# Query pairs one loop step later, and the feed of the bursts with more room at both ends of sweep two

## The chip, the cores and the metric

One core of a Trainium2 chip. The time is the device time of one launch in microseconds (us); the runs shown are medians over several executions. The engines are TensorE (PE; its weight loads are listed apart as PEld), VectorE (DVE), ScalarE (ACT), GpSimd (POOL) and SyncE (SP), which here only issues DMAs.

## The reference

x is 2048 rows of 512 values, all float32.

```python
qkv = x @ wqkv                                   # 32 heads of 16
pq, pk = q @ w_phi, k @ w_phi                    # per head 16 x 16
phi_q = concat(softmax(pq), softmax(-pq))        # 32 features
phi_k = concat(softmax(pk), softmax(-pk))
kv, z = phi_k^T v, sum over rows of phi_k        # over all 2048 rows
a = ((phi_q kv) / (phi_q z + 1e-6)) @ wo
h = relu(x @ w1 + b1); h = h * h                 # 1792 hidden columns
b = h @ w2 + b2
g = sigmoid(sum(x * gate_w))
out = g * a + (1 - g) * b
```

kv and z need all rows before the first query can be used; this divides the kernel into two sweeps over the rows.

## The kernel before, in words

A float32 product is made of three fp32r matmuls (mm3): each operand is split into a high part, which ACT rounds (`xh`, `hh`, `oh`, ...), and a low part, which DVE subtracts (`xl`, `hl`, `ol`, ...).

The rows are taken in 4 blocks of 512, the hidden columns in 14 chunks of 128. Each sweep passes over all blocks with 7 of the 14 chunks. So the main loop has 2 x 4 x 7 = 56 steps t. In each, PE does one `u` group of 12 matmuls (do_up, for the chunk that is needed two steps on, LAG = 2) and one `d` group of 12 (down, into four PSUM accumulators); ACT and DVE make the squared relu between them (hidden). At the end of a block the accumulators are added into rows (L597), the evictions below: in sweep one these go out as `part`, in sweep two they are added to what sweep one left, and either finish or meet the attention part.

All other work hangs in between at half steps: at(s, f, ...) puts f into half step s, where 2t comes ahead of the `u` group of step t and 2t + 1 between `u` and `d`. A framework then orders each engine's queue by these program positions and its own estimate of when operands and buffers are free, with some pieces (exps, the splits of `oh` and `ol`, the evictions) given a higher priority.

Sweep one (half steps 0 to 55) carries, beside the FFN, for each 128 rows the products `k` and `v`, the exponentials of `k`, and phi_k^T v (`kvps`, which holds one PSUM bank, so that one bank is left for all else). Near its end the weights for the queries are made: do_fold("q", k) at half steps 49 to 52, each a small product in that one bank (`foldq`) and a split (`wqh`, `wql`). Also near its end the next block's x rows, the first of sweep two, are split (x_ready, `xh` and `xl`, two 128-row pieces in a half step), from buffers that x_fetch has loaded; do_w loads and splits `wo` (`woh`, `wol`).

Sweep two (56 to 111) carries the queries. A pair p of row chunks goes through

- do_q, twice, two half steps apart: the product `q`, exponentials on DVE and ACT, the denominator (POOL makes `ez`, DVE `dz`, `den`), the scaled features, and transposed: DVE transposes 32 x 32 blocks into `tb`, and 16 copies bring these to their place in `phiT`, 4 by ACT and 12 by DMAs that SP issues (L303). `phiT` has one buffer, so the copies of a pair wait for the burst of the pair before.
- do_n, ten half steps after the first do_q: the burst `num`, 32 small matmuls on `phiT` into two PSUM banks, and the split of the result (`oh`, `ol`). The first two matmuls of the burst run ahead of the other 30.
- finish, twice, from twelve half steps after the first do_q: the product `att` with `wo`, and its addition to the row (L490).

`q`, `num` and `att` share two PSUM banks in turn. do_x(b) loads and splits the x rows of the later blocks at half steps 63, 72 and 82. A block of sweep two ends at 69, 83, 97 and 111.

```python
for p in range(NB * NC // 2):
    n, s = 2 * p, 54 + 6 * p
    q, late = divmod(n, NC)[0], p == NB * NC // 2 - 1
```

Of the kernel before, what the change touches and what calls it, by code (L numbers as in the profile page):

```python
# [20 lines left out]
NB = S // SB  # L21
NC = SB // P
# [10 lines left out]
def tile_gated_mix(ctx: ExitStack, tc: tile.TileContext, xT, xn, wqT, wkT, wphi, wv, wo, w1, b1, w2, b2, gw, out):  # L33
# [464 lines left out]
    SL = 2 * NFH  # L498
    steps = {}

    def at(slot, f, *a):
        steps.setdefault(int(slot), []).append(lambda: f(*a))
# [13 lines left out]
    for b in range(NB):  # L516
        for c in range(NC):
            s = b * SL + 3 * c - 3 if b else 3
            at(s, gate_load, b * NC + c)
            at(s + 3 if b else 8 + c, gate_chunk, b * NC + c)  # L520
        at(b * SL + 4, x_fetch, b + 1)
        for k in range(NK):
            at(b * SL + 7 + k // 2, x_ready, b + 1, k)
        for c in range(NC):
            n = b * NC + c
            s = 5 + 2.9 * n
            at(s, do_k, b, c)
            at(s + 2, do_v, b, n, c)
            if c % 2:
                at(s + 5, do_kv, n - 1)  # L530
# [9 lines left out]


    for p in range(NB * NC // 2):
        n, s = 2 * p, 54 + 6 * p
        q, late = divmod(n, NC)[0], p == NB * NC // 2 - 1
        at(s + 12 - 2 * late, finish, n, n % NC)
        at(s + 13 - 2 * late, finish, n + 1, n % NC + 1)
        at(s, do_q, NB + q, n, n % NC)
        at(s + 2, do_q, NB + q, n + 1, n % NC + 1)
        at(s + 10 - 2 * late, do_n, p)
    for b, slot in enumerate((7, 2, -2)):  # L550
        at((NB + b) * SL + slot, do_x, NB + b + 1)

# [12 lines left out]
    for t, (sw, b, i) in enumerate(work_list):  # L565
# [17 lines left out]
        for c in range(NC):  # L583
            n = b * NC + c
# [62 lines left out]
```

## Time and profile before

| | |
|---|---|
| median of 3 runs | 526.96 us (526.89 to 527.18) |
| the profiled execution | 527.2 us, of which the span from first to last instruction is 525.4 |
| busy, share of the span | PE 98%, PEld 79%, DVE 69%, ACT 45%, POOL 15% |
| granted TensorE clock | 0.999 of full speed |
| DMA queue of SP and ACT | 30328 packets, 44.20 MB, 26.7% of 16 engines' span |

Read it so: matmuls are pipelined and their ends are modelled, so one matmul row is shown with about 390 ns while the next one starts 227 ns later; PE's 98% says that it hardly ever lay idle. A row of the timeline is start, duration, engine, line, operation, output <- inputs, shapes, count, and in brackets the idle time of the engine before it with what ended it.

### The profile page before, as it was taken

What the parts mean: (1) busy time and instruction counts of PE and PEld (TensorE: products, weight loads), DVE (VectorE), ACT (ScalarE), POOL (GpSimd) and SP (SyncE); (2) the same over time, 40 slices, a digit from 0 to 9 for tenths busy, and PEclk for the clock granted to TensorE, in tenths of its full rate; (3) what the DMA queues carried; (4) which work ended last, traced back from release to release, by engine and by line L of the source; (5) the groups of instructions that cost most, each with busy time, mean ns of one, the idle gap of its engine ahead of it and who ended that gap; (6) DMA issues with size and microseconds to landing.
All of it is one profiled execution on the core that took longest, in us unless ns stands there. A gap on an engine that the chain in (4) does not pass through costs nothing.

```text
span 525.4 us, 8895 instructions
## 1 busy us (share of the span) xinstructions
PE 517.2 (98%) x3462; PEld 415.9 (79%) x3462; DVE 360.5 (69%) x606; ACT 236.5 (45%) x405; POOL 78.1 (15%) x60
## 2 busy tenths in 40 slices
PE   8999999999999999999999999999999999999997
PEld 3887888888888888888788878787878878787785
DVE  3569764463636646765879897997788887779323
ACT  5665534344334444354754473553434352535230
POOL 1001211111111111210103121112021111112000
PEclk9999999999999999999999999999999999999999
DMA  8844131120201031521255113234103311022102
GB/s 290 308 142 142 61 93 48 42 81 21 94 9 41 8 133 42 160 72 31 80 167 197 41 42 121 68 105 133 45 13 111 109 32 30 24 91 81 48 1 80
DMA packets 30834, 45.16 MB, mean 86 GB/s; under 512 B 5704, under 2 KB 12360, under 8 KB 30792
## 3 DMA queue, kind: packets, MB, share of 16 engines
q1 hardware_dynamic: 30328, 44.20, 26.7%
q8 instruction: 27, 0.44, 0.3%
q10 hardware_dynamic: 432, 0.39, 0.2%
q14 instruction: 15, 0.12, 0.1%
q0 software_dynamic: 32, 0.01, 0.0%
HBM read 29.89 MB, written 8.39 MB: 73 GB/s over the span
## 4 chain that ended last, share of the span: by engine, by line
PE 73%; DVE 12%; SPq 4%; issue 3%; ACT 2%; DMA 2%; POOL 2%; DVEq 0%; ACTq 0%; POOLq 0%
PE u L70 7%; PE u L72 7%; PE u L71 7%; PE d L71 7%; PE d L72 7%; PE d L70 7%; SPq L303 4%; PE v L70 3%; PE v L71 2%; PE v L72 2%; PE k L70 2%; PE k L72 2%; PE k L71 2%; PE att L70 2%; POOL ez L277 2%
## 5 line engine op out<-in xcount | busy, mean ns | idle before, releaser
L349 ACT ACTIVATE r<-u,b1c 128x512 f32<-128x512 f32 x56 | 38.5, 687 | 140.1 <-PE u L72 139.7
L70 PE MATMUL d<-w2h,hh 128*128 128x512 f32 x224 | 87.4, 390 | 0.0
L71 PE MATMUL d<-w2l,hh 128*128 128x512 f32 x224 | 87.4, 390 | 0.0
L72 PE MATMUL d<-w2h,hl 128*128 128x512 f32 x224 | 87.2, 389 | 0.0
L70 PE MATMUL u<-xh,w1h 128*128 128x512 f32 x220 | 86.9, 395 | 0.0
L72 PE MATMUL u<-xh,w1l 128*128 128x512 f32 x220 | 85.9, 390 | 0.0
L71 PE MATMUL u<-xl,w1h 128*128 128x512 f32 x220 | 85.7, 390 | 0.0
L65 DVE TENSOR_TENSOR hl<-r,hh 128x512 fp32r<-128x512 f32 x56 | 43.1, 769 | 53.4 <-ACT hh L62 53.2
L277 POOL TENSOR_TENSOR ez<-e,z 128x512 f32<-128x512 f32 x32 | 41.4, 1315 | 188.7 <-ACT e L249 164.5
L258 POOL TENSOR_TENSOR e<-e,r 128x1024 f32<-128x1024 f32 x16 | 34.5, 2158 | 206.6 <-DVE r L254 131.7
L252 DVE TENSOR_REDUCE sm<-e 128x64 f32<-128x1024 f32 x32 | 39.0, 1218 | 32.9 <-ACT e L249 32.9
L70 PEld LDWEIGHTS u<-xh,w1h 128*128 128x128 f32 x220 | 41.3, 188 | 12.1 <-ACT hh L62 1.6
L70 PEld LDWEIGHTS d<-w2h,hh 128*128 128x128 f32 x224 | 42.1, 188 | 8.7
L72 PEld LDWEIGHTS d<-w2h,hl 128*128 128x128 f32 x224 | 42.1, 188 | 8.7
L71 PEld LDWEIGHTS d<-w2l,hh 128*128 128x128 f32 x224 | 42.1, 188 | 8.6
L72 PEld LDWEIGHTS u<-xh,w1l 128*128 128x128 f32 x220 | 41.3, 188 | 9.3 <-DVE w1l L65 0.7
L71 PEld LDWEIGHTS u<-xl,w1h 128*128 128x128 f32 x220 | 41.3, 188 | 8.2
L249 ACT ACTIVATE e<-e 128x1024 f32<-128x1024 f32 x32 | 33.7, 1055 | 21.8 <-DVE e L247 17.3
L301 ACT ACTIVATE phiT<-tb 32x256 f32<-32x256 f32 x64 | 26.5, 414 | 34.5 <-DVE tb L295 33.8
L62 ACT ACTIVATE hh<-r 128x512 fp32r<-128x512 f32 x56 | 35.3, 630 | 1.5
L350 ACT ACTIVATE r<-r 128x512 f32<-128x512 f32 x56 | 35.2, 629 | 1.2
L597 DVE SCALAR_TENSOR_TENSOR row<-d,rest,row 128x512 f32<-128x512 f32 (+1 forms) x33 | 22.4, 732 | 6.2 <-PE d L72 6.1
(100 smaller groups left out, 872.3 us busy)
## 6 DMA issues: line engine op xcount, KB each, us to landing
in<-in_w SPq DMA_DIRECT2D x24, 256.0 KB, 2.7
phiT<-tb SPq DMA_DIRECT2D x192, 32.0 KB, 1.8
xin<-in_xT SPq DMA_DIRECT2D x20, 256.0 KB, 4.6
xn<-in_xn SPq DMA_DIRECT2D x16, 256.0 KB, 2.8
part<-row SPq DMA_DIRECT2D x16, 256.0 KB, 3.0
row<-part SPq DMA_DIRECT2D x16, 256.0 KB, 3.1
out<-row SPq DMA_DIRECT2D x15, 256.0 KB, 2.3
in<-in_xT SPq DMA_DIRECT2D x12, 256.0 KB, 4.3
```

Source lines behind the costliest of these rows:

```text
L62: i = nc.scalar.activation(hi, src, AF.Copy)
L65: st["low"] = elo.tensor_tensor(lo, src, hi.bitcast(F32), ALU.subtract)
L70: nc.tensor.matmul(o, ah[:, sa], bh[:, sb], start=first, stop=False)
L71: nc.tensor.matmul(o, ah[:, sa], bl[:, sb], start=False, stop=False)
L72: return nc.tensor.matmul(o, al[:, sa], bh[:, sb], start=False, stop=last)
L249: nc.scalar.activation(ef, ef, AF.Exp)
L252: nc.vector.tensor_reduce(sm, e3, AX.X, ALU.add)
L258: eng.tensor_tensor(e3, e3, w.unsqueeze(2).to_broadcast([P, 2 * H, DH]), ALU.mult)
L277: nc.gpsimd.tensor_tensor(ez[:, hs, :], e3[:, hs, :], zbc[half], ALU.mult)
L301: nc.scalar.activation(dst, src, AF.Copy)
L349: nc.scalar.activation(r, ps, AF.Relu, bias=b1c[:, fc:fc + 1])
L350: nc.scalar.activation(r, r, AF.Square)
```

## The change

- x_fetch and x_ready of the last block of sweep one (which loads the first rows of sweep two) are placed two half steps sooner: x_fetch at 44 and not 46, x_ready at 47 and 48 and not 49 and 50.
- Pair 0: its do_q stay at 54 and 56; its burst goes from 64 to 66, its finish from 66 and 67 to 68 and 69.
- Pairs 1 to 6: all their parts two half steps later (pair 1: do_q 62 and 64, burst 72, finish 74 and 75).
- Pair 7: do_q from 96 and 98 to 98 and 100; burst from 104 to 107, finish from 106 and 107 to 109 and 110.

No operation is added or removed.

```diff
@@ -518,9 +518,10 @@
-        at(b * SL + 4, x_fetch, b + 1)
-        for k in range(NK):
-            at(b * SL + 7 + k // 2, x_ready, b + 1, k)
+        early = 2 if b == NB - 1 else 0
+        at(b * SL + 4 - early, x_fetch, b + 1)
+        for k in range(NK):
+            at(b * SL + 7 - early + k // 2, x_ready, b + 1, k)
@@ -540,13 +541,14 @@
     for p in range(NB * NC // 2):
-        n, s = 2 * p, 54 + 6 * p
+        n, s = 2 * p, 54 + 6 * p + 2 * (p > 0)
         q, late = divmod(n, NC)[0], p == NB * NC // 2 - 1
-        at(s + 12 - 2 * late, finish, n, n % NC)
-        at(s + 13 - 2 * late, finish, n + 1, n % NC + 1)
+        t = s + 12 - late + 2 * (p == 0)
+        at(t, finish, n, n % NC)
+        at(t + 1, finish, n + 1, n % NC + 1)
         at(s, do_q, NB + q, n, n % NC)
         at(s + 2, do_q, NB + q, n + 1, n % NC + 1)
-        at(s + 10 - 2 * late, do_n, p)
+        at(t - 2, do_n, p)
```

## The prediction

> **What bounds the kernel now.** I read the page first, then the waits of TensorE (PE), then a table of the eight bursts, the chain around the one place where a fold waits, and last the rows of the queues that feed the two worst bursts.
>
> ```profile
> span 525.4 us, 8895 instructions
> PE 517.2 (98%) x3462; PEld 415.9 (79%) x3462; DVE 360.5 (69%) x606; ACT 236.5 (45%) x405; POOL 78.1 (15%) x60
> PEclk9999999999999999999999999999999999999999
> ```
>
> PE is busy for 98% of the span, at full granted clock. Nothing but PE time can be won: either fewer matmuls, which this change does not bring (it removes and adds no instruction), or fewer holes in PE's stream. So I look for the holes, in the view of the waits:
>
> ```profile
> PE num L314 <- DMA phiT<-tb: 1.6, 2, 0.8
> PE foldq L171 <- DVE wql L65: 0.8, 1, 0.8
> ```
>
> Us in total, times, and the longest. Behind the warm-up, twice a burst (`num`, the 32 small matmuls of `numer`) waits for the copies of phiT, once a fold waits for VectorE (DVE). A busy PE is not yet a PE at its pace, so the next rows (six of the eight bursts, in the view by stretches) take a burst from its first matmul to the start of the `u` matmuls behind it; the second column is what it costs PE. The last three columns are the granted clock, the DMA share and GB/s.
>
> ```profile
> 306.20:308.62 2.42, 1.64 (x33) 0.70 (x32) 2.42 (x3) 2.39 (x6) 2.23 (x2) 1.00 0.11 31
> 392.94:393.96 1.02, 1.02 (x33) 0.49 (x32) 0.96 (x1) 1.02 (x4) 0.85 (x1) 1.00 0.00 0
> 421.39:423.13 1.74, 1.64 (x33) 0.70 (x33) 1.71 (x3) 1.14 (x2) 0.00 (x0) 1.00 0.00 0
> 451.01:452.04 1.03, 1.03 (x34) 0.49 (x33) 0.96 (x1) 0.56 (x2) 0.85 (x1) 1.00 0.00 0
> 479.46:480.49 1.03, 1.03 (x34) 0.49 (x33) 1.03 (x2) 0.21 (x1) 1.03 (x2) 1.00 0.00 0
> 497.03:499.50 2.47, 1.64 (x34) 0.70 (x33) 0.00 (x0) 0.00 (x0) 0.00 (x0) 1.00 0.09 23
> ```
>
> An undisturbed burst costs 1.03 us. The first costs 2.42, the last 2.47, the fifth (421.39) 1.74: losses of 1.39, 1.44 and 0.71. With the fold's hole these are the places where the order of the steps can be worth anything.
>
> **Part 1: x_ready of the last block of sweep one, two half steps sooner.** The chain that led to the fold:
>
> ```profile
> 249.60 0.54 DVE xl L65
> 251.96 1.88 DVE xl L65 x3
> 253.84 0.60 DVE w2l L65
> 254.44 1.21 DVE wol L65 x2
> 255.65 0.61 DVE wql L65
> ```
>
> DVE works off four `xl`, one `w2l` and two `wol` before the `wql` that empties the one free PSUM bank; the third fold starts 0.84 us late, though ScalarE (ACT) had delivered the `wqh` long before:
>
> ```profile
> 256.30 1.16 PE L171 MATMUL foldq<-row 128*128 128x128 f32 x8 [0.84 <-DVE wql L65]
> 253.88 0.60 ACT L62 ACTIVATE wqh<-foldq 128x512 fp32r<-128x512 f32 x1 [1.25 <-PE foldq L171]
> ```
>
> `wqh` ended at 254.48. With the four `xl` gone, `w2l` and `wol` are done by then and `wql` takes 254.48 to 255.16; PE is free for the fold at 256.30 - 0.84 = 255.46. Gain: 0.84. Bounds: none, and 0.84.
>
> Where do the rows go? Half steps 47 and 48, behind the hidden block whose `hh` ends at 235.17:
>
> ```profile
> 234.54 0.63 ACT L62 ACTIVATE hh<-r 128x512 fp32r<-128x512 f32 x1
> 237.28 0.58 ACT L443 ACTIVATE vext<-v 128x512 f32<-128x512 f32 x1
> 240.42 0.69 DVE L65 TENSOR_TENSOR w2l<-in,w2h 128x512 fp32r<-128x512 f32 x1 [2.47 <-ACT w2h L62]
> 242.48 0.69 DVE L244 TENSOR_REDUCE mx<-k 128x32 f32<-128x512 f32 x1 [1.36 <-PE k L72]
> 249.60 4.24 DVE L65 TENSOR_TENSOR xl<-xin,xh 128x512 fp32r<-128x512 f32 x4
> 233.74 2.25 POOL L258 TENSOR_TENSOR e<-e,r 128x1024 f32<-128x1024 f32 x1 [11.42 <-DVE gate L225]
> 249.31 2.17 POOL L258 TENSOR_TENSOR e<-e,r 128x1024 f32<-128x1024 f32 x1 [13.34 <-DVE r L254]
> ```
>
> DVE sits idle there for 2.47 + 1.36 = 3.83 us before the reduction of `k` at 242.48, ACT for 2.1 between 235.17 and 237.28. The four `xl` took 4.24 in their old place, because the first ran beside the POOL operation of 249.31; the three behind it took (253.84 - 251.96) / 3 = 0.63 each. In the new place POOL is done at 235.99, so I take 4 x 0.68 = 2.72 (0.68 is `wql`'s 0.61 and its lead-in), which fits into 3.83: cost nothing. If they took 4.24 again, 0.41 of it would push the reduction, and with one bank the folds behind it: that is the bound above (+0.41); below, nothing is won there.
>
> The Trainium skill, page "SBUF — State Buffer", section "Who interferes with whom", says that a DVE instruction with two SBUF inputs and a GpSimd instruction that reads SBUF shut each other out for a whole instruction, whoever issues first. The rows agree: the first `xl` starts at 249.60 and the second only at 251.96, half a microsecond after POOL's end at 251.48. By this rule the moved rows cost 2.72 and the sum stands; by the rows taken as they come (4.24) it would be 0.41 worse. The rule also speaks against the change: what comes next on DVE at 249.6 (`w2l`, also two SBUF inputs) is now the one shut out until 251.5. It has room: `w2l` and two `wol`, 3 x 0.68 from 251.5, end at about 253.5, a microsecond before `wqh` ends.
>
> The matching move of x_fetch (half step 46 to 44) costs and brings nothing: its four loads left the SP queue when their buffers came free, some 50 us before they are read.
>
> ```profile
> 182.35 2.01 SPq L131 DMA_DIRECT2D xin<-in_xT  x4
> ```
>
> **Part 2: the first burst two half steps later.** q0 and q1 stay, the other pairs and the first burst move to two half steps later; before the first burst lie the same projections q2 and q3 and one more `u`, `d` pair. What the burst waits for is set by SP, not by PE:
>
> ```profile
> 289.43 1.24 DVE L295 STREAM_TRANSPOSE tb<-e 128x1024 f32<-128x1024 f32 x1
> 290.70 26.09 SPq L303 DMA_DIRECT2D phiT<-tb  x36
> 306.20 0.62 PE L314 MATMUL num<-phiT,kvb 64*32 64x256 f32 x2
> 307.60 1.09 PE L314 MATMUL num<-phiT,kvb 64*32 64x256 f32 x30 [0.78 <-DMA phiT<-tb]
> ```
>
> q0's transposition ends at 290.67. SP then issues 24 copies for q0 and q1 at (26.09 + 0.03) / 36 = 0.73 each at most, 0.64 where it runs without a pause (15.30 / 24, below), and when the last has landed the other 30 matmuls start, at 307.60: 1.4 after PE's arrival at 306.20. One more `u`, `d` pair is 2 x 2.72 = 5.44 us (next fence: 12 matmuls of `d` from 483.34 to 486.06). The hole is covered with 5.44 - 1.4 = 4.0 to spare. Gain: 1.39. Since the cover is so wide I take no bound below it but that of the rivals. The queue behind: phiT has one buffer, so SP's copies for q2 wait for the burst, now later by the same two half steps as q2 itself; PE's way from burst to burst stays the same, and there 24 copies (15.3) fit into 28.5 (451.01 to 479.46).
>
> **Part 3: the last burst.** First the rows of its feed, with the second transposition of a pair in four places:
>
> ```profile
> 483.34 0.39 PE L70 MATMUL d<-w2h,hh 128*128 128x512 f32 x1
> 486.06 0.39 PE L70 MATMUL att<-woh,oh 128*128 128x512 f32 x1
> 481.65 15.30 SPq L303 DMA_DIRECT2D phiT<-tb  x24
> 487.86 1.25 DVE L295 STREAM_TRANSPOSE tb<-e 128x1024 f32<-128x1024 f32 x1
> 496.36 1.88 DMA phiT<-tb
> 431.66 1.25 DVE L295 STREAM_TRANSPOSE tb<-e 128x1024 f32<-128x1024 f32 x1
> 460.24 1.24 DVE L295 STREAM_TRANSPOSE tb<-e 128x1024 f32<-128x1024 f32 x1
> 407.11 1.25 DVE L295 STREAM_TRANSPOSE tb<-e 128x1024 f32<-128x1024 f32 x1
> 500.26 1.29 DVE L65 TENSOR_TENSOR ol<-num,oh 128x512 fp32r<-128x512 f32 x2 [5.16 <-ACT oh L62]
> ```
>
> From the start of burst seven (479.46) PE needs now 1.03 + 6 x 2.72 = 17.35 to the last burst (two `u`, two `d`, two `att`; 17.57 measured), and the copies allow it at 498.48, that is 19.02 after. Now the last burst is at half step 107 and burst seven at 102: one more `u` lies between, 1.03 + 7 x 2.72 = 20.07. If the copies keep their 19.02, the wait is gone with 1.05 to spare. They keep it if the second transposition ends no later than 20.07 - (11 x 0.64 + 0.04 + 1.88 + 0.24) = 10.9 after burst seven's start (twelve issues, landing, and the 0.24 from 498.24 to 498.48). Now it ends at 489.11 - 479.46 = 9.65; a pair earlier at 461.48 - 451.01 = 10.47; behind burst five at 432.90 - 421.39 = 11.51; behind burst four, with x rows and evictions on DVE, at 408.36 - 392.94 = 15.42. With the last block's x long loaded, 9.65 to 10.5 is the likely place. Gain: 1.44. Bounds: 1.44, and a loss of 3.04 (15.42 - 10.9 = 4.5 of waiting in place of 1.44).
>
> Behind the last burst the cover of its split shrinks: now `u` and `d`, 5.44; then only `d`, 2.72, since the last `u` goes ahead of the burst. The split's last `ol` ends at 501.55, 2.05 after the burst's end (499.50), and only the last third of an `att` product needs it. If ACT does the hidden block first (three operations like the `hh` of 234.54, some 0.65 each, less the 1.03 of the burst), it is up to 0.9 later, still before the use at 2.72 + 1.36 + 0.45. Cost 0, at most 0.2. The final additions, stores and the tail behind 521.5 are as before: the last 24 `d` still come last.
>
> **Part 4: the other pairs.** Relative to their own bursts nothing moves, but the x rows (half steps 63, 72, 82) and the evictions at a block's end (69, 83, 97) come two half steps earlier in their pair. That bears on burst five, which has lost 0.71:
>
> ```profile
> 421.22 0.68 DVE L247 TENSOR_TENSOR e<-mn,q 128x512 f32<-128x512 f32 x1
> ```
>
> Its first two matmuls ran at 421.39, the others only when this subtraction had emptied the second bank (421.90). DVE was behind because x rows (82) and evictions (83) had come on top of the fourth pair's end; now these come before burst four, and burst five gets 5.4 us longer to recover, while burst three has the x rows of 72 at its own half step. I let the 0.71 move to another burst: 0. Bounds: 0.71 won; 1.42 lost if bursts three and four both wait as five did.
>
> **Sum.** 0.84 + 1.39 + 1.44 = 3.67. The profiled execution took 527.2, so 523.5; the median of the runs shown, 526.96, lies 0.24 lower: 523.3. A measurement of this kernel can tell about 0.2% (1.05 us) from no change.
>
> **Rivals.**
> - *The last burst still waits.* SP needs 15.3 for 24 copies whatever PE does; a second transposition at 11.5, as behind burst five, leaves 0.6 of the wait, and one at 12.3 leaves all 1.44. For it: only 1.05 is to spare. Against: 9.65 and 10.47 in the two pairs before. Time 523.9 to 524.7.
> - *The backlog of DVE only moves.* The fold loses 0.41 to the moved rows, bursts three and four wait 0.71 each: 523.3 + 0.41 + 1.42 = 525.1. For it: DVE is the second busiest engine (69%), and burst five shows the mechanism. Against: bursts four, six and seven show no such wait (1.03).
> - *Nothing is won.* Both together: 525.1 + 1.44 = 526.5, inside 0.2% of now; the change would then not do what it says.
> - *Slower.* The last pair's second transposition is as late as behind burst four (15.42): PE waits 4.5 at the last burst, with no `u` left to put there. 526.96 - 0.84 - 1.39 + 3.04 = 527.8. It turns slower than now when the transposition ends more than 14.6 after burst seven. Against: no x rows and no evictions fall between half step 97 and the last burst. The Trainium skill, page "TensorE: Matmul & The Clock Gate", section "Why this matters for your kernels", warns of gaps of more than about 3 us between bursts, after which PE runs at half clock; no hole of the stream here is that long (the longest wait is 0.8), so no run shows what it would add.
>
> **How the numbers follow.** The forecast, with fold, first and last burst gone, 523.3: 0.58, own range 522.6 to 524.0. The last burst still waits: 0.17. The backlog moves: 0.13. Nothing won: 0.06. Slower or even: 0.06. Low end: 523.3 less burst five's 0.71 and the pause of 0.3 in the `d` behind it, 522.2. High end: the second rival and half a last wait, 525.8; that leaves out the last two cases and a little of the second. Faster by over 0.2%: 0.58 + 0.17 + 0.10 = 0.85. Within: 0.10. Slower: 0.05.
>
> **What would show it.** Right: no wait of PE for `wql` or phiT; `xl` of xin at 235 to 242 in four pieces of 0.68; first and last burst at 1.03; the last SP copy landed before the last burst. Wrong: a `num` in two pieces (2, then 30) anywhere, with phiT or a DVE subtraction of `q` as its releaser; a `foldq` behind DVE; an `att` behind `ol` after the last burst; a second transposition later than 10.9 after burst seven.

## The result and the profile after

The changed kernel takes 523.73 us (median of 4 runs, 523.64 to 523.96) against 527.03 for the kernel before: ratio 0.9938, 95% interval 0.9926 to 0.9950, a gain of 3.3 us. Its profiled execution took 523.66, the span is 521.9. Measured a second time, beside its own variants, it gave 0.9936 (0.9924 to 0.9948).

The page and the waits of PE:

```profile
span 521.9 us, 8898 instructions
PE 515.3 (99%) x3462; PEld 415.2 (80%) x3462; DVE 362.6 (69%) x606; ACT 237.3 (45%) x405; POOL 79.0 (15%) x60
PE att L70 <- DVE row L490: 0.3, 1, 0.3
PE kvt L476 <- DVE row L465: 0.3, 1, 0.3
```

The rows that led the list behind the warm-up, `num` behind phiT and `foldq` behind `wql`, are gone; two small new ones stand in their place. Five of the eight bursts, each from its first matmul to the first matmul behind it (a `u`; behind the last burst a `d`); the second column is its cost:

```profile
310.56:311.59 1.03, 1.03 (x34) 0.49 (x33) 1.03 (x2) 1.00 (x3) 0.79 (x1) 1.00 0.18 66
368.42:369.95 1.53, 1.53 (x34) 0.70 (x33) 0.35 (x2) 1.14 (x2) 0.00 (x0) 1.00 0.55 159
397.47:398.49 1.02, 1.02 (x33) 0.49 (x32) 1.02 (x3) 0.41 (x1) 1.02 (x2) 1.00 0.03 10
425.92:426.94 1.02, 1.02 (x33) 0.48 (x33) 0.96 (x1) 0.55 (x2) 0.85 (x1) 1.00 0.00 0
503.10:504.12 1.02, 1.02 (x33) 0.48 (x33) 0.00 (x0) 0.89 (x2) 0.00 (x0) 1.00 0.07 16
```

First (310.56) and last (503.10) burst cost 1.03 and 1.02 in place of 2.42 and 2.47; the fifth (425.92) lost its 0.71, and the third (368.42) now has 0.5. The place around the third fold, on DVE and PE, with the moved rows:

```profile
236.09 1.28 DVE L65 TENSOR_TENSOR xl<-xin,xh 128x512 fp32r<-128x512 f32 x2
237.91 0.68 DVE L65 TENSOR_TENSOR xl<-xin,xh 128x512 fp32r<-128x512 f32 x1
238.58 0.68 DVE L65 TENSOR_TENSOR xl<-xin,xh 128x512 fp32r<-128x512 f32 x1
249.25 2.42 DVE L65 TENSOR_TENSOR w2l<-in,w2h 128x512 fp32r<-128x512 f32 x1
251.60 1.28 DVE L65 TENSOR_TENSOR wol<-in,woh 128x512 fp32r<-128x512 f32 x2
253.94 0.69 DVE L65 TENSOR_TENSOR wql<-foldq,wqh 128x512 fp32r<-128x512 f32 x1 [1.06 <-ACT wqh L62]
254.71 1.13 PE L171 MATMUL foldq<-row 128*128 128x128 f32 x8
```

The four `xl` stand between 236.1 and 239.3, 0.6 to 0.7 each. DVE now waits 1.06 for ACT ahead of `wql`, where it had been behind. The fold shows no idle time.

The span is 3.5 shorter, 0.3 of it in the opening, which no step of the change touches. Counted from matmul start to matmul start, the eight bursts together gave 11.76 - 8.70 = 3.06, the fold 1.0 (1.23 from the start ahead of it, now 0.23), the pause ahead of the `att` behind burst five 0.3. Four places lost again. Burst three lost 0.5, which is within the 8.70. The twelve `d` that have the two transpositions `kvt` among them lost 0.3: 3.25 before, from 264.77 to 268.02, and 3.54 now, from 263.39 to 266.93. Two `att` behind the first burst lost 0.2 (317.35) and 0.5 (326.12). Two of these places, on PE:

```profile
266.44 0.41 PE L476 MATMUL kvt<-ident,row 128*128 128x128 f32 x2 [0.26 <-DVE row L465]
326.12 0.50 PE L70 MATMUL att<-woh,oh 128*128 128x512 f32 x1 [0.32 <-DVE row L490]
```

Outside the bursts that makes 1.3 won and 1.0 lost, so 3.4 in all; without its opening the span shows 3.2.

### The profile page after: what moved, and what is told of

Read it like the earlier page. It is cut to its first block, busy times and chain, and to the rows that moved or that the text cites. A ratio compares the mean times of both kernels' runs of the same rounds, so it can differ in the third digit from the quotient of the medians.

```text
span 521.9 us, 8898 instructions
## 1 busy us (share of the span) xinstructions
PE 515.3 (99%) x3462; PEld 415.2 (80%) x3462; DVE 362.6 (69%) x606; ACT 237.3 (45%) x405; POOL 79.0 (15%) x60
## 4 chain that ended last, share of the span: by engine, by line
PE 92%; DVE 3%; DMA 2%; ACT 1%; issue 1%; POOL 0%; SPq 0%; DVEq 0%; POOLq 0%
PE u L70 9%; PE u L72 9%; PE d L70 9%; PE d L72 9%; PE u L71 9%; PE d L71 9%; PE v L70 3%; PE k L70 3%; PE v L71 3%; PE v L72 3%; PE k L72 3%; PE k L71 3%; PE att L70 3%; PE att L72 3%; PE att L71 3%; PE q L70 2%
## 5 line engine op out<-in xcount | busy, mean ns | idle before, releaser
L279 DVE TENSOR_REDUCE dz<-ez 128x64 f32<-128x1024 f32 x16 | 19.4, 1210 | 9.5 <-POOL ez L277 9.5
```

## The experiments

**One part alone: the x rows.** The two lines for x_fetch and x_ready, the rest as before.

> The kernel before with the x rows of the last block of sweep one (x_fetch, x_ready) two half steps sooner and nothing else. Theory (each part closes its own hole in TensorE's stream, and the holes add): the third fold's wait for VectorE (0.84 us) is gone, first and last burst keep 2.4 each, fifth 1.7; time 0.8 to 1.0 less than before, ratio about 0.9983. Rival (the gains come from the later pairs alone, the x rows only change what VectorE works at when): no change, ratio 1.000, and the wait of the fold comes back at another fold or at the v product.

Measured: 526.23 against 527.22, ratio 0.9979 (0.9970 to 0.9988), a gain of 1.1 (0.6 to 1.6). In its waits `foldq` is missing; the first burst still costs 2.35, the fifth 1.74, the last 2.47. `kvt` now waits 0.3 for DVE, as in the changed kernel, so that new loss belongs to this part: of the fold's 1.0 it takes 0.3, and the span is 0.7 shorter. The theory holds.

**One part alone: the first burst.**

```diff
-        at(s + 12 - 2 * late, finish, n, n % NC)
+        t = s + 12 - 2 * late + 2 * (p == 0)
+        at(t, finish, n, n % NC)
...
-        at(s + 10 - 2 * late, do_n, p)
+        at(t - 2, do_n, p)
```

> The kernel before with the first pair's burst at half step 66 and its finish at 68 and 69, all other pairs and the x rows where they were. Theory: the first burst stops waiting for SyncE's copies (2.42 to 1.03), 1.4 less, ratio about 0.9974; the last burst keeps its 2.47. The other pairs need not move for that. Rival (the other pairs had to move because q2's copies wait for the first burst, phiT has one buffer): the second burst, now only four half steps behind the first, waits in its place, since 24 copies take 15.3 and TensorE's way to it is 1.03 + 6 x 2.72 = 17.4 less what the copies need to land: ratio 1.000.

Measured: 527.97, ratio 1.0024 (1.0014 to 1.0034): slower. Neither expectation held. The first burst did cost 1.02 and the second burst did not wait. But the third pair's first product, at the same half step as the burst, came less than one `u` group behind it and needed a bank that the burst had just filled. Timeline of PE and DVE, then PE's stretches around it (the last three columns: granted clock, DMA share, GB/s):

```profile
316.35 0.67 PE L70 MATMUL q<-wqh,xh 128*128 128x512 f32 x1 [1.90 <-DVE ol L65]
314.49 1.21 DVE L258 TENSOR_TENSOR e<-e,w 128x1024 f32<-128x1024 f32 x1
315.62 0.68 DVE L65 TENSOR_TENSOR ol<-num,oh 128x512 fp32r<-128x512 f32 x1
```

```profile
312.00:314.00 2.00, 2.00 (x23) 1.40 (x8) 2.00 (x7) 1.47 (x4) 0.00 (x0) 1.00 0.37 107
314.00:316.30 2.30, 0.45 (x2) 0.03 (x1) 2.30 (x4) 1.26 (x3) 0.00 (x0) 1.00 0.88 268
316.30:318.00 1.70, 1.65 (x4) 1.36 (x5) 1.70 (x2) 0.51 (x2) 0.00 (x0) 0.57 0.68 216
318.00:320.00 2.00, 2.00 (x6) 1.52 (x6) 0.03 (x1) 1.15 (x3) 0.00 (x0) 0.52 0.20 53
320.00:322.00 2.00, 2.00 (x11) 1.64 (x10) 1.01 (x2) 0.10 (x1) 0.00 (x0) 1.00 0.18 49
```

PE stood still for 1.90 until DVE had emptied the bank, 2.06 more from start to start than usual. That is 0.7 more than the 1.39 won at the burst, and the median is 0.75 longer than before. In the profiled execution (529.37) the granted clock then fell to half for 3.4 us, so that the twelve matmuls behind took 4.43 from start to start and not 2.72. Four of the eleven executions (529.1 to 530.0) have the same lower mean clock, 0.997; the other seven took 527.7 to 528.0. So the later pairs had to move too, for the two banks that `q` and `num` share, not for phiT.

**One part alone: the last burst**, one half step later (`t = s + 12 - late`, finish at t, do_n at t - 2), the rest as before.

> The kernel before with the last pair's burst one half step later (105, behind the last but one u group) and its finish at 107 and 108; all else as before. Theory: burst seven to last burst 1.03 + 7 x 2.72 = 20.1 against the 19.0 that the copies need: the last burst costs 1.03 and not 2.47, 1.4 less, ratio about 0.9973. Rival (the wait only moves on to the split behind the burst, whose cover shrinks): att waits for ol by 0.5 to 1.4, ratio 0.998 to 1.000.

Measured: 525.56, ratio 0.9968 (0.9955 to 0.9980), a gain of 1.7. The last burst:

```profile
499.88 1.09 PE L314 MATMUL num<-phiT,kvb 64*32 64x256 f32 x32
```

In one piece, and no wait of `att` behind it. Here the theory holds and the rival falls.

**The shift without the room**: all eight pairs two half steps later, distances inside the pairs as before (`s = 56 + 6 * p`).

> The kernel before with all eight pairs two half steps later, the first two query products and the first burst too, all distances inside a pair as before (last burst at 106), x rows as before. Theory (it is the distance of the burst from its copies, not the place in the sweep): first and last burst still cost 2.4 and 2.5, the fold still waits; burst five's 0.7 goes or moves to burst three; ratio 0.998 to 1.001. Rival (the later place alone frees the queues): both waits go, ratio 0.995.

Measured: 529.20, ratio 1.0030 (1.0020 to 1.0039), slower than expected. Eight of the eleven executions took 529.0 to 529.5 at a mean clock of 0.995 to 0.997, three 527.3 to 527.8 at 0.999 to 1.000; the profiled one is of the three. The first two rows are the first burst and the `att` behind it, the others the last burst:

```profile
311.06 1.09 PE L314 MATMUL num<-phiT,kvb 64*32 64x256 f32 x32
318.51 0.50 PE L70 MATMUL att<-woh,oh 128*128 128x512 f32 x1 [0.69 <-DVE ol L65]
501.54 0.62 PE L314 MATMUL num<-phiT,kvb 64*32 64x256 f32 x2
503.98 1.09 PE L314 MATMUL num<-phiT,kvb 64*32 64x256 f32 x30 [1.82 <-DMA phiT<-tb]
```

The theory was half wrong: the first burst does not wait, though its distance from its products is the old one. For it the place in the sweep counts: SP begins its copies at 292.16, only 1.5 later than the 290.70 before, although the products stand a whole step of the loop later and the burst comes 4.9 later. The last burst waits, as its distance says, but 1.82 and not the old 0.83: its second transposition ends 10.97 after burst seven (483.98), and before it was 9.65. So the shift of the pairs itself makes that feed later.

**The changed kernel with the last burst's old distance** (`- 2 * late` in place of `- late`):

> The changed kernel with the last burst at 106 and its finish at 108 and 109, the distance from its query products that it had before. Theory (the copies need 20.1 us from burst seven: second transposition at 10.97 in the changed kernel and 9.1 of issue and landing; TensorE is there after 1.03 + 6 x 2.72 = 17.4): the last burst costs 1.03 + 2.7 = 3.7, as the 3.46 of the kernel shifted without room; 2.4 to 2.7 more than the changed kernel, ratio to before about 0.998; where the hole drops the granted clock, as in the runs of the shifted kernel that took 1.6 more, another 1.6. Rival (the copies need only what they needed before, 19.0): 1.4 more than the changed kernel, ratio 0.996.

Measured: 527.89, ratio 1.0002 (0.9992 to 1.0012): without this one half step the gain is gone, though fold and first burst are as in the changed kernel. The second part of the burst, then PE's stretches up to its end and the 4.44 behind it:

```profile
502.89 1.09 PE L314 MATMUL num<-phiT,kvb 64*32 64x256 f32 x30 [1.82 <-DMA phiT<-tb]
```

```profile
500.00:503.92 3.92, 2.10 (x36) 0.81 (x34) 0.00 (x0) 0.00 (x0) 0.00 (x0) 1.00 0.15 38
503.92:508.36 4.44, 4.44 (x18) 3.53 (x13) 1.29 (x2) 1.08 (x2) 0.00 (x0) 0.62 0.00 0
```

The burst started at 500.46, so it cost 3.46 (3.7 expected). The twelve `u` behind it ran at a mean granted clock of 0.62 and took 1.7 longer than the usual 2.72. The eight runs with a mean clock of 0.995 to 0.997 took 527.7 to 528.1, the three at 0.998 to 1.000 took 526.6 to 526.7: 1.3 us hang on the clock, the rest on the hole. The theory holds, in both of its cases.

**Two queues**: the old order of steps; in the first and the last pair ScalarE issues 8 of the 12 copies.

```diff
-                    nc.sync.dma_start(dst, src)
+                    (nc.scalar if share and (j + r) % 2 else nc.sync).dma_start(dst, src)
```

> The kernel before, order of steps untouched, but of the 12 copies of phiT of each query product in the first and last pair ScalarE issues 8 and SyncE 4. Theory (what both bursts wait for is SyncE's 0.64 us per issue): first and last burst cost 1.03, 2.8 less, ratio about 0.9947, less what ScalarE's issuing holds up (8 x 0.6 = 4.8 us per product, at a ScalarE that is busy 45% of the time). Rival for the first burst (the sums z arrive late, the chain through POOL and VectorE sets the end): with half the issue time in SyncE the first burst still waits.

Measured: 525.2, ratio 0.9964 (0.9949 to 0.9980), both bursts in one piece without moving any step:

```profile
306.69 1.09 PE L314 MATMUL num<-phiT,kvb 64*32 64x256 f32 x32
496.37 1.09 PE L314 MATMUL num<-phiT,kvb 64*32 64x256 f32 x32
```

SyncE's issuing is what both bursts waited for. Of the 2.8 expected 1.9 arrived (1.1 to 2.7). In the profiled execution the bursts give back all 2.8, but its opening, which the edit does not touch, is 0.6 longer. Three of the seven executions took 526.6 to 526.8, the others 524.6 to 525.2; two of the three had a mean clock of 1.000, and why they are longer stays open.

**The first products moved along** (`s = 56 + 6 * p` in the changed kernel, burst and finish where they are):

> The changed kernel with the first pair's query products two half steps later as well (56 and 58), burst and finish as in the changed kernel (66, 68, 69). Theory A, now (the first burst's feed begins when the sums z are there, so neither the burst nor its copies care where the products stand; but the products' work on VectorE then lies nearer to the burst): first burst 1.03, att behind it waits for ol by 0.7 as in the kernel shifted without room; 0.5 to 0.9 more than the changed kernel, ratio to before about 0.995. Rival B (distance from product to burst counts, 10 half steps in place of 12): first burst 2.4 again, ratio 0.9965.

Measured: 524.74, ratio 0.9945 (0.9931 to 0.9959). The first burst is in one piece, `att` behind it waits 0.69 for `ol`, the stream loses 0.85 there (0.2 in the changed kernel): theory A. So leaving q0 and q1 in their place is not for the burst: it keeps their work on DVE clear of the split behind it. Against the changed kernel's own ratios (0.9938, 0.9936) the time is not told apart; the rows are.

**The place of two small losses.** First `kvt`: the four copies of kvps get the higher priority.

> The changed kernel with the four copies of kvps out of PSUM given the higher priority, so that they stand together ahead of hl in VectorE's queue, as they did before the change. Theory (the transposition kvt waits for the fourth copy, 0.56 lost in the stream of d at 263.4 since the change): that 0.56 goes to 0.2 or less, ratio to before 0.993, 0.3 to 0.5 less than the changed kernel. Rival (hl comes 0.4 later and a d group waits instead): no change against the changed kernel.

Measured: ratio 0.9926 (0.9913 to 0.9939), which is not told apart from the changed kernel's 0.9938 and 0.9936. In the rows the theory holds: the copies stand together again, `kvt` no longer waits, and the twelve `d` with it take 3.24, as before the change. So the loss that went is 0.3 and not the 0.56 that the expectation names.

```profile
264.12 1.72 DVE L466 COPY row<-kvps 17x256 f32<-17x256 f32 x4 [1.85 <-PE kvps L267]
```

Then, on top of that, the x rows of half step 72 (`enumerate((7, 2, -2))`) at three other places, beside the changed kernel on the same chip.

> The kernel e11_kv_copies_first with the x rows of the third block of sweep two split at half step 70 in place of 72. Theory (burst three costs 1.57 because these rows' xl stand before the subtraction that empties its second bank): ahead of burst two, with two query products' work less behind them, they leave burst three at 1.03, 0.5 less than e11; burst two, 2 half steps behind them, stays at 1.03. Rival (VectorE's backlog only moves): burst two waits by about the same 0.5.

> The kernel e11_kv_copies_first with the x rows of the third block of sweep two split at half step 75 in place of 72. Theory: xl stands behind the first product of its pair and right ahead of burst three; the subtraction has the higher priority and goes first, but the backlog stays: burst three 1.0 to 2.0, time the same as e11 within 0.5. Rival: burst three is free and the wait turns up at burst four.

> The kernel e11_kv_copies_first with the x rows of the third block of sweep two split at half step 67 in place of 72, right behind burst one and ahead of the evictions of 69. Theory: burst three at 1.03, but att behind burst one waits longer for VectorE (0.48 in the changed kernel) by up to 1: about the same time as e11. Rival: both waits go, 1.0 less than e11.

> The changed kernel itself, beside the others on one chip: ratio to before 0.9938 again, the fifth burst at 1.03, the third at 1.5, 0.3 to 0.5 above a kernel that differs from it by the place of the kvps copies alone.

Measured: 523.02, 523.24, 523.80, and 524.12 for the changed kernel; ratios 0.9916 (0.9903 to 0.9929), 0.9924 (0.9911 to 0.9936), 0.9930 (0.9917 to 0.9943) and 0.9936 (0.9924 to 0.9948). Burst three at 70, at 75 and in the changed kernel, then burst two at 67:

```profile
368.47:369.53 1.06, 1.06 (x33) 0.59 (x33) 0.04 (x1) 1.06 (x2) 0.00 (x0) 1.00 0.37 139
368.56:369.58 1.02, 1.02 (x33) 0.48 (x33) 1.02 (x2) 0.41 (x1) 1.02 (x2) 1.00 0.85 229
369.19:370.75 1.56, 1.56 (x33) 0.70 (x33) 0.38 (x2) 1.13 (x2) 0.00 (x0) 1.00 0.57 162
339.70:341.77 2.07, 1.64 (x33) 0.70 (x32) 1.93 (x7) 1.13 (x2) 0.00 (x0) 1.00 0.80 290
```

At 70 the theory holds, in the rows: burst three costs 1.06, burst two 1.02. At 75 both expectations missed: the wait is gone and does not come back at burst four or any other. At 67 neither named what came: burst three is free, but burst two costs 2.07 (0.43 idle between its first two matmuls and the rest), and the `att` wait is gone. The version with 70 has the lowest time of all, 4.3 us under the kernel before; its interval and the changed kernel's still touch.

## Why the prediction was right, step by step

- Part 1, the fold: 0.84 forecast, the row shows it gone, the part alone is worth 1.1 (0.6 to 1.6). The `xl` ran in 0.6 to 0.7 each at the forecast place. Also as forecast, `w2l` was shut out beside POOL's operation (2.42 at 249.25, the operation from 248.95 to 251.12) and `wql` still came in time. Missed: with this part an `hl` stands between the copies of kvps, which costs 0.3 at `kvt`. I had looked for what the rows displace up to the folds and not beyond.
- Part 2, the first burst: 1.39 forecast and shown. The reason, SP's issuing, is confirmed by the two queues; the last copy landed at 306.35, 4.2 ahead of the burst (4.0 forecast). But I priced "the other pairs" at nothing because their distances stay. The run with the first burst alone showed that their move is a condition: without it the product behind the burst waits for its bank. Nor was the move free: the `att` wait at 326.12 is also there in the kernel shifted without room (0.31 idle), and not in the kernels whose pairs stayed in place.
- Part 3, the last burst: 1.44 forecast and shown, but with less room than I wrote, and some luck. The limit for the second transposition was worked out as 10.9 after burst seven, and a later one was named as a sign of being wrong; it ended at 10.97, past that limit and later than the 9.65 to 10.5 that I took:

```profile
482.81:483.83 1.02, 1.02 (x33) 0.49 (x32) 0.45 (x1) 1.02 (x2) 0.34 (x1) 1.00 0.00 0
492.54 1.24 DVE L295 STREAM_TRANSPOSE tb<-e 128x1024 f32<-128x1024 f32 x1
484.08 17.20 SPq L303 DMA_DIRECT2D phiT<-tb  x24
```

  PE itself came at 503.10, 20.29 after burst seven and not 20.07, and the last copy, issued at about 484.08 + 17.20 - 0.59 = 500.69, could start the burst 1.88 + 0.24 later, at 502.81: 0.3 to spare, where I had written 1.05. The two kernels with the old distance agree: there the copies let the other 30 matmuls start 20.0 after burst seven (503.98 - 483.98 and 502.89 - 482.89). What was mis-sized is the place of that transposition, taken over from kernels whose pairs were not moved: with the pairs in place it ends at 9.65 (in the run with the last burst alone too, 489.25 - 479.60), with the pairs moved at 10.97, so the shift itself used 1.3 of the room. What on DVE makes it later was not tested. The gain came, but the rival "the last burst still waits" was 0.3 away. With the old distance the same feed cost 3.46 and, in most runs, the clock.
- The split behind the last burst cost nothing, as forecast: `att` at 506.97 shows no wait.
- Part 4: burst five's 0.71 moved to another burst, 0.5 at burst three, by the x rows of 72, as named there.
- The sum: 3.67 forecast, 3.3 measured. From 3.67 the three new losses take 0.3 at `kvt` and 0.2 and 0.5 at `att`; burst five and the pause behind it gave up 1.0, of which burst three took 0.5; the fold gave 1.0 and not 0.84: 3.67 - 1.0 + 0.5 + 0.16 = 3.3. None of the three losses was in the forecast; that burst five's part made up for half of them is luck, since it was put at nothing.
- The slower rival was priced without the clock. Had it come true, its hole of 4.5 could have cost the clock as well; an estimate from the hole of 1.8, whose next twelve matmuls took 1.7 more, is another 1.7. No run has such a hole.

## What to carry to other kernels

Where one engine is busy for 98% of the span, make a table of the same work's cost at each of its repeats. The odd ones out show where time can be won (here the bursts gave 3.1 us, the fold 1.0), and each has its own feeder with an issue rate and an end that can be computed to some tenths of a microsecond. A part of a change that seems to win nothing by itself can be what lets another part win: here moving the first burst alone was slower, since the next product stood behind it for a PSUM bank. And work that keeps its distances inside its own group still moves against everything else: check its feed anew. Spare room below half a microsecond is worth finding out by one run on either side: one half step at the last burst decided between 523.7 and 527.9.

## What the runs showed of the hardware

A hole of 1.8 to 1.9 us in PE's stream was enough to drop the granted clock to half for 3.4 us, by their mean clock in 8 of 11 runs of the kernel with the old last distance and in 4 of 11 with the first burst alone. The twelve matmuls behind it then took 1.7 us more, almost the price of the hole itself. In the profiled executions with holes of up to 0.9 and bursts of 2.4 to 2.6, the granted clock stayed at 1.00 around them. The Trainium skill, page "TensorE: Matmul & The Clock Gate", section "Why this matters for your kernels", names gaps of more than about 3 us; here shorter ones did it: the limit for this kernel lies between 0.9 and 1.8 of idle time.

The length of the hole alone does not decide. The clock was at half from 316.52 to 319.94 with the first burst alone, and from 504.04 to 507.45 with the old last distance, 3.41 us each time; in the first of these traces the next change, at 528.15, comes 61 such steps later. In the 3.41 us ahead of these, which held the whole hole, PE was busy for 1.51 and 1.59. The profiled execution of the kernel shifted without room has the same hole of 1.82, and its clock stayed at 1.00. There the records of the clock change only at 523.92, behind the last matmul; counted back from there in steps of 3.41, the hole falls into two stretches (500.03 to 503.44 and 503.44 to 506.86), in which PE was busy for 2.13 and 2.88. A reading that fits all three, and that no run tested on its own: the clock is set every 3.41 us by how busy PE was in the stretch before, so that the same hole costs the clock in one run and not in the next.
